# q of all four tiles ahead of k, smaller first transfers, and later z2 weights, in the opening of a fused attention and gMLP kernel

## The chip, the cores and the metric

One core of one Trainium2 chip. The metric is device time in microseconds (us) of one execution. A kernel is run several times; a timed comparison alternates it with the kernel before on the same chip. One execution of each is also profiled. Its span, as the profile prints it, is 1.7 to 1.9 us shorter than the same execution's device time.

Three engines matter here: TensorE (PE in the profile; PEld is its weight load), VectorE (DVE) and ScalarE (ACT). SyncE (SP) issues nearly all DMAs.

## The reference

With `x` of 2048 rows by 512 columns, normalised to `xn`, the result is the sum of `x` and two branches.

```python
xn = layernorm(x)
# A: sliding dilated attention, 32 heads of 16, window 8, dilation 2
q, k, v = xn @ wqkv;  o = softmax(q . k[window] / 4) v[window];  A = o @ wo
# B: gMLP
z = gelu(xn @ w_in);  z1, z2 = halves of z (688 columns each);  z2 = layernorm(z2)
B = (z1 * (w_sp @ z2 + b_sp)) @ w_out
out = x + A + B
```

## The kernel before

All of the program is ordered by hand. The 16 row tiles (128 rows each) form four "blocks" of four tiles (`j` is the block, `tb` the tile in it). The opening loads x and weights, normalises block 0, transposes it on TensorE and projects q and k of it. Then it does the same for block 1, whose last two tiles are transposed by DMA instead. After that the first matmuls with the z2 weights follow, and from there on a fixed list of steps.

```python
for tb in range(2):                       # first two x tiles, half on each DMA-issuing engine
    load_x0(SP, tb, 0); load_x0(A, tb, 1)
for tb in range(2, TB):
    A.dma_start(xall[:, 0, tb], xblk[0][:, tb])
load_wqk(SP, 0, 0, 2)                     # q weights, two transfers of 256 rows
load_wqk(SP, 0, 2, 4)
SP.dma_start(xall[:, 1, 0:2], xblk[1][:, 0:2])
load_wqk(SP, 1)                           # k weights, 512 KB
SP.dma_start(xall[:, 1, 2:4], xblk[1][:, 2:4])
for j in range(2, 4):
    SP.dma_start(xall[:, j], xblk[j])
SP.dma_start(w_z2[:], ...)                # z2 weights, 688 KB
# ... cut ...
def tr_copy(i, pt, c0=0, c1=C):           # ScalarE takes a transposed tile out of PSUM
    A.copy(xnT[:, c0:c1, i*P:(i+1)*P], pt[:, c0:c1, :])
def tr_dma(i):                            # or the tile is transposed by DMA
    SP.dma_start_transpose(xnT[:, :, i*P:(i+1)*P], xall[:, j, tb, :])
# qk_part(pq, j, m, b0, b1): projection m of block j for its tiles b0..b1; m 0,1 are q, m 2,3 are k
# ... cut ...
warm_up(10)                               # 10 matmuls of 512 columns on zeros
# ... cut: block 0, tiles 0 to 3 normalised; tiles 0 and 1 transposed ...
qk_part(pqs[0], 0, 0, 0, 2, kcs=range(2)); qk_part(pqs[0], 0, 0, 0, 2, kcs=range(2, 4))
tr_copy(t0[2], tr(t0[2]))
qk_part(pqs[1], 0, 1, 0, 2, (0,))
tr_copy(t0[3], tr(t0[3]))
qk_part(pqs[1], 0, 1, 0, 2, (1,))
qk_part(pqs[2], 0, 2, 0, 2)               # k of tiles 0 and 1: needs the k weights
# ... cut: statistics of block 1 ...
for n in range(2):
    qk_part(pqs[n], 0, n, 2, 4)           # q of tiles 2 and 3
    qk_copy(pqs[n], 0, n)
# ... cut: rest of block 0, transposes of block 1, block 1's projections, first z matmuls ...
```

Of the kernel before, what the change touches and what calls it, by code (L numbers as in the profile page):

```python
# [15 lines left out]
P = 128  # L16
# [3 lines left out]
TB = 4  # L20
TBS = 512
C = D // P
# [5 lines left out]
F = 1376  # L28
FH = 688
# [42 lines left out]
def kernel(  # L72
# [13 lines left out]
    V = nc.vector  # L86
# [3 lines left out]
    SP = nc.sync  # L90
# [3 lines left out]
    xblk = x2.rearrange("(b j p) d -> j p b d", b=TB, j=4)  # L94
# [9 lines left out]
    xall = r_x[:, 0:4 * TB * D].rearrange("p (j b d) -> p j b d", j=4, b=TB)  # L104
# [33 lines left out]
    xnT = sb.tile([P, C, S], BF16, name="xnT")  # L138
    w_z2 = sb.tile([P, C, FH], BF16, name="w_z2")
# [30 lines left out]
    def load_wqk(E, s, k0=0, k1=C):  # L170
        E.dma_start(wqk[:, s, k0:k1],
                    A_wqkv[:, s * D:(s + 1) * D].rearrange("(k p) f -> p k f", p=P)[:, k0:k1])
# [3 lines left out]
        load_x0(A, tb, 1)  # L176
    for tb in range(2, TB):
        A.dma_start(xall[:, 0, tb], xblk[0][:, tb])
    load_wqk(SP, 0, 0, 2)
    load_wqk(SP, 0, 2, 4)  # L180
    SP.dma_start(xall[:, 1, 0:2], xblk[1][:, 0:2])  # L181
    load_wqk(SP, 1)
    SP.dma_start(xall[:, 1, 2:4], xblk[1][:, 2:4])
    for j in range(2, 4):
        SP.dma_start(xall[:, j], xblk[j])
    SP.dma_start(w_z2[:], B_w_in[:, FH:F].rearrange("(k p) f -> p k f", p=P))


    V.memset(warm[:, 0:P], 0.0)
# [17 lines left out]
    def ln_stats(i, parts=1):  # L207
        j, tb = i % 4, i // 4
        w = D // parts
        for h in range(parts):  # L210
            V.bn_stats(stats[:, i, 6 * h:6 * h + 6], xall[:, j, tb, w * h:w * h + w])  # L211
        V.bn_aggr(mv[:, i, :], stats[:, i, 0:6 * parts])

    def ln_sqrt(sl):
        A.activation(rstd[:, sl], mv[:, sl, 1], ACT.Sqrt, bias=eps_t[:])

    def ln_recip(sl):
        V.reciprocal(rstd[:, sl], rstd[:, sl])

    def ln_apply(i):  # L220
        j, tb = i % 4, i // 4
        V.tensor_scalar(xall[:, j, tb, :], xall[:, j, tb, :], mv[:, i, 0:1], rstd[:, i:i + 1],
                        ALU.subtract, ALU.mult)

    def tr(i):
        j, tb = i % 4, i // 4
        pt = ps_aux.tile([P, C, P], BF16, name="pt", tag="aux")
        for c in range(C):
            PE.transpose(pt[:, c, :], xall[:, j, tb, c * P:(c + 1) * P], ident[:])  # L229
        return pt  # L230

    def tr_copy(i, pt, c0=0, c1=C):
        A.copy(xnT[:, c0:c1, i * P:(i + 1) * P], pt[:, c0:c1, :])

    def tr_dma(i):
        j, tb = i % 4, i // 4
        SP.dma_start_transpose(xnT[:, :, i * P:(i + 1) * P], xall[:, j, tb, :])
# [70 lines left out]
    def qk_part(pq, j, m, b0, b1, ccs=(0, 1), p0=None, kcs=range(C)):  # L308
        sd, c0 = m // 2, 2 * (m % 2)
        p0 = b0 if p0 is None else p0  # L310
        xv = xnT[:].rearrange("p k (b j t) -> p k b j t", b=TB, j=4)
        for cc in ccs:
            for kc in kcs:
                PE.matmul(pq[:, cc, p0 * P:(p0 + b1 - b0) * P], wqk[:, sd, kc, c0 + cc:D:C],  # L314
                          xv[:, kc, b0:b1, j, :], start=(kc == 0), stop=(kc == C - 1))

    def qk_copy(pq, j, m, b0=0, b1=TB, p0=None):
        sd, c0 = m // 2, 2 * (m % 2)
        p0 = b0 if p0 is None else p0
        if sd == 0:  # L320
            dst = qs[:, j, c0:c0 + 2, b0 * P:b1 * P].rearrange("p c (b t) -> p c b t", b=b1 - b0)
        else:
            dst = ks[:, c0:c0 + 2, HALO:HALO + S].rearrange("p c (b j t) -> p c b j t", b=TB, j=4)[:, :, b0:b1, j, :]
        cast = A.copy(dst, pq[:, :, p0 * P:(p0 + b1 - b0) * P].rearrange("p c (b t) -> p c b t", b=b1 - b0))  # L324
        if sd == 1:
            for i in k_reads[j]:
                tc.declare_no_dep(cast.ins, i, reason="other token columns of the same rows")
            k_casts[j].append(cast.ins)

    def qk_tile():  # L330
        return ps_mm.tile([P, 2, TBS], F32, name="pq", tag="mm")
# [219 lines left out]
    def blk(j):  # L551
        return [4 * tb + j for tb in range(TB)]

    def col(i):
        return slice(i, i + 1)
# [9 lines left out]
    def ln_tile(i):  # L565
        ln_recip(col(i))
        ln_apply(i)

    t0, i1 = blk(0), blk(1)
# [5 lines left out]
    for n in range(2):  # L575
        ln_tile(t0[n])
    tr_copy(t0[0], tr(t0[0]))
    pt1 = tr(t0[1])
    tr_copy(t0[1], pt1, 0, 2)
    tr_copy(t0[1], pt1, 2, 4)  # L580
    warm_up(1)
    warm_up(1, 2)
# [5 lines left out]
    pqs = [qk_tile() for _ in range(3)]  # L588
    qk_part(pqs[0], 0, 0, 0, 2, kcs=range(2))
    qk_part(pqs[0], 0, 0, 0, 2, kcs=range(2, 4))  # L590
    tr_copy(t0[2], tr(t0[2]))
    qk_part(pqs[1], 0, 1, 0, 2, (0,))
    tr_copy(t0[3], tr(t0[3]))
    qk_part(pqs[1], 0, 1, 0, 2, (1,))
    qk_part(pqs[2], 0, 2, 0, 2)
    for n in range(2):
        ln_stats(i1[n])
    ln_sqrt(slice(1, 8, 4))
    ln_stats(i1[2])
    ln_recip(slice(1, 8, 4))  # L600
    ln_apply(i1[0])
    ln_apply(i1[1])
    ln_stats(i1[3])
    for n in range(2):
        qk_part(pqs[n], 0, n, 2, 4)
        qk_copy(pqs[n], 0, n)
    ln_sqrt(slice(9, 16, 4))
    ln_stats(i2[0])
    ln_recip(slice(9, 16, 4))
    for n in range(2, 4):  # L610
        ln_apply(i1[n])
        tr_dma(i1[n])
    qk_part(pqs[2], 0, 2, 2, 4, (0,))
    tr_copy(i1[0], tr(i1[0]))
    qk_part(pqs[2], 0, 2, 2, 4, (1,))
    tr_copy(i1[1], tr(i1[1]))
    qk_copy(pqs[2], 0, 2)
    pq3 = qk_tile()
    qk_part(pq3, 0, 3, 0, 4)
    qk_copy(pq3, 0, 3)  # L620
    for n in range(1, 4):
        ln_stats(i2[n])
    ln_sqrt(blk_cols(2))
# [7 lines left out]
    pqs = [qk_tile() for _ in range(3)]  # L631
# [79 lines left out]
```

## Time and profile before

| | before |
|---|---|
| timed, median of 3 | 203.11 us (202.99 to 203.35) |
| the profiled execution | 204.07 us, span 202.2 us |
| TensorE busy | 97% of the span |
| chain of waits | 92% TensorE |

From the page of the kernel before, the busy times (us, share of the span, instructions) and the engines of the chain of waits:

```profile
...
PE 196.5 (97%) x1667; PEld 124.5 (62%) x1667; DVE 186.4 (92%) x269; ACT 106.8 (53%) x174; POOL 4.0 (2%) x14
...
PE 92%; DMA 5%; DVE 1%; issue 0%; SPq 0%
...
```

The chain of waits of the kernel before in the first 45 us (start, length, what):

```profile
...
3.64 6.73 DMA r_w<-in_A_wqkv_dram
...
10.42 3.25 PE pq L314 x28
13.67 0.22 PE pt L229 x4
13.89 0.44 PE pq L314 x4
14.33 0.22 PE pt L229 x4
14.55 4.35 PE pq L314 x32
18.90 0.87 PE pa L314 x8
19.77 3.49 PE pq L314 x32
23.27 3.50 PE pz L243 x24
...
```

What TensorE waited for in the kernel before from 6 to 24 us (total, times, longest):

```profile
...
PE pq L314 <- DMA r_w<-in_A_wqkv_dram: 0.9, 1, 0.9
...
```

The chain reads as follows: the k weights were issued at 3.64 us and took 6.73 us to land. From 10.42 us TensorE works without a break through the projections (`pq`, `pa`), and reaches the first z matmul (`pz`) at 23.27 us. Before 10.42 us it stood 0.9 us, waiting for these weights. A chain that is TensorE from there to the end says that only the opening can be shortened.

### The profile page before, as it was taken

Reading aid. Unit: us, or ns where it says so; the run is one execution under the profiler, and the core shown is the slowest. Engines: PE = TensorE matmul, PEld = TensorE weight load, DVE = VectorE, ACT = ScalarE, POOL = GpSimd, SP = SyncE. Lnnn points to the kernel's source line nnn. Section 1 sums busy time; section 2 is a strip of 40 time slices with the busy share of each in tenths; the row PEclk is TensorE's granted clock in tenths of the full one; section 3 lists DMA queues with packets and bytes.
Section 4 is the critical chain, followed back from the end, with each engine's and each line's share of the span. In section 5 each row is a group of like instructions: output and inputs, shape, how many; then the busy total and the mean of one; then the engine's idle time right before and its main releaser. Section 6 shows DMA issues by size and latency. Waiting matters only on the chain.

```text
span 202.2 us, 4055 instructions
## 1 busy us (share of the span) xinstructions
PE 196.5 (97%) x1667; PEld 124.5 (62%) x1667; DVE 186.4 (92%) x269; ACT 106.8 (53%) x174; POOL 4.0 (2%) x14
## 2 busy tenths in 40 slices
PE   7799999999999999999999999999999999999994
PEld 2589856646656666666656666644666446664562
DVE  5979799999999999999979999999999999999814
ACT  3565999889999886081383285134712152131400
POOL 3000000400000000000000000000000000000000
PEclk9999999999999999999999999999999999999999
DMA  5982557000895000759939908990243996059373
GB/s 154 339 272 55 104 104 249 0 0 0 133 201 87 0 3 0 135 167 231 220 81 199 223 5 203 201 211 7 77 104 85 249 188 90 0 148 189 84 221 110
DMA packets 66338, 25.91 MB, mean 128 GB/s; under 512 B 56272, under 2 KB 66064, under 8 KB 66064
## 3 DMA queue, kind: packets, MB, share of 16 engines
q1 hardware_dynamic: 65600, 25.19, 55.0%
q10 hardware_dynamic: 720, 0.47, 0.7%
q8 instruction: 13, 0.21, 0.5%
q14 instruction: 5, 0.04, 0.1%
HBM read 10.13 MB, written 2.10 MB: 60 GB/s over the span
## 4 chain that ended last, share of the span: by engine, by line
PE 92%; DMA 5%; DVE 1%; issue 0%; SPq 0%
PE pg L457 37%; PE pz L243 19%; PE pq L314 13%; PE po L535 8%; PE pv L418 7%; PE po L505 6%; DMA r_w<-in_A_wqkv_dram 3%; DMA r_x<-in_A_x_dram 1%; PE pl L368 1%; DVE r_pr L523 1%; PE po L514 1%; PE pb L505 1%; PE pa L314 0%; PE pt L229 0%; SPq L181 0%
## 5 line engine op out<-in xcount | busy, mean ns | idle before, releaser
L457 PE MATMUL pg<-z,r_qk 128*128 128x344 bf16 x448 | 66.6, 309 | 0.0
L457 PEld LDWEIGHTS <-r_qk 128*128 128x128 bf16 x448 | 43.8, 98 | 21.8
L243 PE MATMUL pz<-w_z,xnT 128*128 128x344 bf16 x256 | 40.0, 309 | 0.0
L432 DVE TENSOR_TENSOR r_pr<-r_x,r_w 128x2048 bf16<-128x2048 bf16 x32 | 38.5, 1220 | 0.3
L463 ACT ACTIVATE gs<-pg,b_col 128x688 bf16<-128x688 f32 x16 | 13.2, 834 | 48.2 <-PE pg L457 48.2
L436 DVE TENSOR_TENSOR r_pr<-r_pr 128x2048 bf16<-128x2048 bf16 x28 | 34.1, 1219 | 0.4
L243 PEld LDWEIGHTS <-xnT 128*128 128x128 bf16 x256 | 24.6, 98 | 14.4 <-issue 1.9
L314 PE MATMUL pq<-xnT,r_w 128*128 128x256 bf16 (+1 forms) x176 | 29.0, 316 | 1.0 <-DMA r_w<-in_A_wqkv_dram 0.9
L348 DVE TENSOR_TENSOR r_pr<-r_qk 128x2048 bf16<-128x2048 bf16 x24 | 28.3, 1220 | 0.1
L314 PEld LDWEIGHTS <-r_w 128*128 128x128 bf16 x184 | 20.1, 114 | 8.2 <-DMA r_w<-in_A_wqkv_dram 1.1
L324 ACT CAST r_qk<-pq 128x1024 bf16<-128x1024 f32 (+1 forms) x16 | 15.4, 989 | 2.9 <-PE pq L314 2.9
L535 PE MATMUL po<-r_w,r_uz 128*128 128x512 bf16 x70 | 16.0, 379 | 0.0
L305 ACT ACTIVATE r_uz<-pz 128x688 bf16<-128x688 f32 x16 | 11.7, 742 | 7.3 <-PE pz L243 7.2
L505 PE MATMUL po<-r_lg,r_pr 32*128 32x512 bf16 x224 | 14.5, 375 | 0.0
L518 ACT CAST r_qk<-po 128x512 bf16<-128x512 f32 x12 | 6.4, 589 | 14.7 <-PE po L535 14.6
L418 PE MATMUL pv<-xnT,r_w 128*32 128x512 bf16 x256 | 14.2, 379 | 0.0
L535 PEld LDWEIGHTS <-r_uz 128*128 128x128 bf16 x85 | 8.1, 98 | 9.3 <-issue 1.1
L357 DVE TENSOR_TENSOR r_pr<-r_pr 128x4096 bf16<-128x4096 bf16 x6 | 13.6, 2287 | 0.0
L211 DVE BATCH_NORM_STATS2 stats<-r_x 128x6 f32<-128x512 bf16 (+1 forms) x18 | 10.9, 613 | 2.2 <-DMA r_x<-in_A_x_dram 2.2
L267 ACT ACTIVATE junk<-z 128x688 bf16<-128x688 bf16 x16 | 12.4, 776 | 0.1
L418 PEld LDWEIGHTS <-r_w 128*32 128x32 bf16 x256 | 9.5, 138 | 4.4
L261 ACT ACTIVATE z<-pz 128x688 bf16<-128x688 f32 x16 | 11.8, 737 | 0.8 <-PE pz L243 0.7
(83 smaller groups left out, 175.4 us busy)
## 6 DMA issues: line engine op xcount, KB each, us to landing
r_lg<-in_A_wo_dram SPq DMA_DIRECT2D x8, 256.0 KB, 3.9
r_qk<-in_A_x_dram SPq DMA_DIRECT2D x12, 128.0 KB, 2.3
out_dram<-r_qk SPq DMA_DIRECT2D x12, 128.0 KB, 2.8
w_z<-in_B_w_in_dram SPq DMA_DIRECT2D x2, 688.0 KB, 5.4
r_w<-in_A_wqkv_dram SPq DMA_DIRECT2D x2, 512.0 KB, 5.4
r_x<-in_A_x_dram SPq DMA_DIRECT2D x2, 512.0 KB
r_w<-in_B_w_out_dram SPq DMA_DIRECT2D x1, 640.0 KB, 5.7
r_w<-in_A_wqkv_dram SPq DMA_DIRECT2D x2, 256.0 KB, 4.5
```

What stands on the lines that cost most here:

```text
L243: PE.matmul(pz[:, hh, 0:FHALF], xnT[:, kc, i * P:(i + 1) * P], wz[:, kc, hh * FHALF:(hh + 1) * FHALF], start=(kc == 0), stop=(kc == C - 1))
L314: PE.matmul(pq[:, cc, p0 * P:(p0 + b1 - b0) * P], wqk[:, sd, kc, c0 + cc:D:C], xv[:, kc, b0:b1, j, :], start=(kc == 0), stop=(kc == C - 1))
L324: cast = A.copy(dst, pq[:, :, p0 * P:(p0 + b1 - b0) * P].rearrange("p c (b t) -> p c b t", b=b1 - b0))
L348: prod = V.tensor_tensor(pr[g % 3][:, c].rearrange("p w b t -> p b w t"), q3.unsqueeze(2).broadcast_to([P, TB, 4, P]), k4, ALU.mult)
L357: V.tensor_tensor(pr[g % 3][:, 0:2], pr[g % 3][:, 0:2], pr[g % 3][:, 2:4], ALU.add)
L418: PE.matmul(pv[32 * tb:32 * tb + 32, dd, :], wv[:, kc, 2 * d2 + dd, :], xnT[:, kc, tb * TBS:(tb + 1) * TBS], start=(kc == 0), stop=(kc == ...
L432: V.tensor_tensor(pw_t[n], vp[:, :, off:off + P], a_sb[:, slot_w(w), ts].unsqueeze(1).broadcast_to([P, DH, P]), ALU.mult)
L436: V.tensor_tensor(pw_t[n] if dst is None else dst, pw_t[n], pw_t[m], ALU.add)
L457: PE.matmul(pg[:, hh, 0:FHALF], wsp[n][:, k, :], z2[:, k, hh * FHALF:(hh + 1) * FHALF], start=(k == 0), stop=(k == NT - 1))
L463: A.activation(gs[:], tiles.pop(("g", n))[:, :, 0:FHALF], ACT.Identity, bias=b_col[:, i:i + 1])
L505: PE.matmul(pc, op[32 * tb:32 * tb + 32, d, o * P:(o + 1) * P], wo_r[32 * tb:32 * tb + 32, d, cs], start=(d == 8), stop=False, tile_positi ...
L535: PE.matmul(pc, uT[:, o % 2, m, tb * P:(tb + 1) * P], wout[:, m, cs], start=False, stop=(m == MCH - 3))
```

## The change

Three parts. (1) TensorE takes q of all four tiles of block 0 before any k, so it has work while the k weights travel; k is then done in 512-column matmuls. VectorE takes half of tile 3 out of PSUM, and square roots are done per tile. (2) The q weights and block 1's x come in transfers of 128 rows. (3) The z2 weights are issued behind the two DMA transposes of block 1.

```diff
@@ -176,14 +176,14 @@
         load_x0(A, tb, 1)
     for tb in range(2, TB):
         A.dma_start(xall[:, 0, tb], xblk[0][:, tb])
-    load_wqk(SP, 0, 0, 2)
-    load_wqk(SP, 0, 2, 4)
-    SP.dma_start(xall[:, 1, 0:2], xblk[1][:, 0:2])
-    load_wqk(SP, 1)
-    SP.dma_start(xall[:, 1, 2:4], xblk[1][:, 2:4])
+    for kc in range(C):
+        load_wqk(SP, 0, kc, kc + 1)
+    for tb in range(TB):
+        if tb == 2:
+            load_wqk(SP, 1)
+        SP.dma_start(xall[:, 1, tb], xblk[1][:, tb])
     for j in range(2, 4):
         SP.dma_start(xall[:, j], xblk[j])
-    SP.dma_start(w_z2[:], B_w_in[:, FH:F].rearrange("(k p) f -> p k f", p=P))
 
 
     V.memset(warm[:, 0:P], 0.0)
@@ -231,6 +231,9 @@
 
     def tr_copy(i, pt, c0=0, c1=C):
         A.copy(xnT[:, c0:c1, i * P:(i + 1) * P], pt[:, c0:c1, :])
+
+    def tr_copy_v(i, pt, c0, c1):
+        V.tensor_copy(xnT[:, c0:c1, i * P:(i + 1) * P], pt[:, c0:c1, :])
 
     def tr_dma(i):
         j, tb = i % 4, i // 4
@@ -588,36 +591,38 @@
     pqs = [qk_tile() for _ in range(3)]
     qk_part(pqs[0], 0, 0, 0, 2, kcs=range(2))
     qk_part(pqs[0], 0, 0, 0, 2, kcs=range(2, 4))
+    qk_part(pqs[1], 0, 1, 0, 2, (0,))
     tr_copy(t0[2], tr(t0[2]))
-    qk_part(pqs[1], 0, 1, 0, 2, (0,))
-    tr_copy(t0[3], tr(t0[3]))
-    qk_part(pqs[1], 0, 1, 0, 2, (1,))
-    qk_part(pqs[2], 0, 2, 0, 2)
+    qk_part(pqs[1], 0, 1, 0, 2, (1,), kcs=range(2))
+    pt3 = tr(t0[3])
+    qk_part(pqs[1], 0, 1, 0, 2, (1,), kcs=range(2, 4))
+    tr_copy_v(t0[3], pt3, 0, 2)
+    tr_copy(t0[3], pt3, 2, 4)
+    qk_part(pqs[0], 0, 0, 2, 4, kcs=range(2))
+    qk_part(pqs[0], 0, 0, 2, 4, kcs=range(2, 4))
+    qk_part(pqs[1], 0, 1, 2, 4)
     for n in range(2):
         ln_stats(i1[n])
-    ln_sqrt(slice(1, 8, 4))
-    ln_stats(i1[2])
-    ln_recip(slice(1, 8, 4))
-    ln_apply(i1[0])
-    ln_apply(i1[1])
-    ln_stats(i1[3])
+        ln_sqrt(col(i1[n]))
     for n in range(2):
-        qk_part(pqs[n], 0, n, 2, 4)
+        ln_tile(i1[n])
         qk_copy(pqs[n], 0, n)
-    ln_sqrt(slice(9, 16, 4))
+    qk_part(pqs[2], 0, 2, 0, 4)
+    for n in range(2, 4):
+        ln_stats(i1[n])
+        ln_sqrt(col(i1[n]))
+    for n in range(2, 4):
+        ln_tile(i1[n])
+        tr_dma(i1[n])
+    SP.dma_start(w_z2[:], B_w_in[:, FH:F].rearrange("(k p) f -> p k f", p=P))
+    tr_copy(i1[0], tr(i1[0]))
+    pq3 = qk_tile()
+    qk_part(pq3, 0, 3, 0, 4, (0,))
+    tr_copy(i1[1], tr(i1[1]))
+    qk_part(pq3, 0, 3, 0, 4, (1,))
+    qk_copy(pqs[2], 0, 2)
+    qk_copy(pq3, 0, 3)
     ln_stats(i2[0])
-    ln_recip(slice(9, 16, 4))
-    for n in range(2, 4):
-        ln_apply(i1[n])
-        tr_dma(i1[n])
-    qk_part(pqs[2], 0, 2, 2, 4, (0,))
-    tr_copy(i1[0], tr(i1[0]))
-    qk_part(pqs[2], 0, 2, 2, 4, (1,))
-    tr_copy(i1[1], tr(i1[1]))
-    qk_copy(pqs[2], 0, 2)
-    pq3 = qk_tile()
-    qk_part(pq3, 0, 3, 0, 4)
-    qk_copy(pq3, 0, 3)
     for n in range(1, 4):
         ln_stats(i2[n])
     ln_sqrt(blk_cols(2))
```

In instruction counts, TensorE has 3318 matmuls and weight loads in place of 3334: eight pairs of weight load and matmul fewer, because the first half of block 0's k is done in 8 matmuls of 512 columns in place of 16 of 256.

## The prediction

> **What bounds the kernel now.** TensorE. The page gives PE 97% of a 202.2 us span, and the chain of waits is 92% PE. In the table by stages PE is full from 15 us until the tail. The only slack a prologue change can win lies before about 10.4 us: in the chain, PE works without a break from 10.42 us, and what it waited for there is the DMA of the k weights (issued at 3.64, landed at 10.37; 0.9 us of PE idle). By then PE has done 16 of block 0's projection matmuls (256 wide).
>
> **Costs read from the trace.** A 256-wide projection matmul 0.11-0.12 us apart (28 took 3.25 us), a 512-wide one 0.22; four transposes 0.22; ScalarE copy of a transposed tile 0.59 us, of half a tile 0.38; cast of 128x1024 1.0; VectorE statistics of a tile about 0.8, apply 0.41; one DMA transpose occupies the issuing queue 1.3 us and lands 2.4 us after its issue; one load issue about 0.45 us.
>
> **What changes.**
> 1. Order of PE: q of all four tiles first (32 matmuls of 256), then k in 512-wide matmuls. So PE has 16 matmuls more that do not need the k weights. I expect tile 3's halves copied at about 9.4 (VectorE) and 9.8 us (ScalarE), q finished near 11.2 us instead of 12.2, and the k weights there before that. From 11.2, k (1.74), two transposes (0.44) and the last k (1.74) end near 15.1 us, where before block 1's projections began at 16.3: 1.2 us won.
> 2. Transfers in 128-row pieces: same bytes in the same order. Eight DMA semaphores are used in turn, so the k-weight load now waits for the third x tile and issues near 5.3 us instead of 3.64. [...] the packet records show it saturated near 350 GB/s from 4.5 us; its turn comes only at about 6.6-7. So I expect it to land still at 10-10.7 us. ([...] here a load's completions spread by over 1 us.)
> 3. The z2 weights (688 KB) issue near 17 us behind block 1's two transposes and land near 21. They are needed at about 22.3 us (23.1 before). About 1 us of slack.
> 4. ScalarE and VectorE: per-tile square roots put the first two tr copies of block 1 near 14.1-15.2, so PE may wait 0.1-0.2 us there. Block 2's normalisation stays where it was (18.8-18.95), so its four DMA transposes still land by about 25.7, just when PE, 1 us earlier, wants them.
>
> VectorE's block 3 normalisation waits for a square root behind PE-paced casts, so the products also start about 1 us earlier. So the gain should survive, less the waits of point 4.
>
> **Predicted**: 202.2 us, 0.9 less; range 201.5 to 203.0. Faster by over 2%: 0.01; within 2%: 0.98; slower by over 2%: 0.01.
>
> **Signs.** No PE wait for the k weights, or under 0.3 us; first block 1 projection at 15.1-15.4 us instead of 16.3; first z matmul at 22.2-22.5 us instead of 23.1; VectorE's first product near 24.3 instead of 25.28; no PE wait for the z2 weights.
>
> **What would make it wrong.** The k weights landing after 11.2 us (late issue starves the queue): each us late costs one. The z2 weights landing after 22.4, or holding up block 2's transposes, gives the gain back at q of block 2. Or later stages tied to VectorE or loads that do not move: then about 203.

Point 2: "it" is the load queue there, and "its turn" that of the k weights. That this turn comes at 6.6-7, behind the loads issued before, was my estimate, and the "10-10.7" rests on it. What the traces of before and after show is this. In both, the last completions of SyncE's loads up to 8 us (10 in before, 13 in after) come in the order of issue. In before the queues moved 323 to 354 GB/s from 4.5 to 6.5 us, at a DMA share of 0.93 to 1.03; the 16 completions of the k weights came from 8.02 to 10.37 us, and TensorE went on at 10.42. The DMA issues name eight semaphores in turn: in after the load of the k weights has that of the third x tile, whose last completion is at 5.51 us, and issues at 5.53. The sum was the 1.2 us won by the order, less the waits of point 4, put at 0.9 us.

## The result, and the profile after

| | before | after |
|---|---|---|
| timed, 6 runs each, same rounds | 203.1 us (202.99 to 203.82) | 204.0 us (203.4 to 204.25) |
| profiled execution, span | 202.2 us | 201.7 us |

The ratio is 1.0034 (95% interval 1.0014 to 1.0054): slower by a third of a percent, where I had forecast 0.9 us less. A ratio is the mean time of one kernel's fast runs over that of the other's of the same rounds, so it is not quite the ratio of the medians quoted.

The two traces point the other way from the times: the span after is 0.5 us shorter. So neither trace shows a typical execution. The profiled execution of before (204.07 us) was above all its six timed ones, and that of after (203.4 us) was the fastest of its six.

The chain of waits after, first 60 us (answering to the one of before):

```profile
...
14.15 0.41 DVE r_x L222
14.57 0.61 DVE stats L211
15.20 0.18 DVE mv L212
15.38 0.09 DVE stats L211
15.47 3.57 DMA xnT<-r_x
19.04 0.05 issue
19.08 3.69 PE pq L317 x32
22.77 3.50 PE pz L246 x24
...
```

TensorE's wait for a DMA after, same stretch and columns as above:

```profile
...
PE pq L317 <- DMA xnT<-r_x: 0.2, 1, 0.2
...
```

The wait for the k weights is gone, as intended. In its place the chain runs over VectorE (`r_x L222`, the normalisation of block 1) into a DMA transpose `xnT<-r_x`, 3.57 us long, that TensorE waits for before the second half of block 1's projections at 19.08 us.

The load queue in the stretch from 5 to 10 us of the kernel before (length, then busy us and instructions of PE, PEld, DVE, ACT, POOL, granted clock, mean busy DMA engines, GB/s):

```profile
...
5.00:10.00 5.00, 3.69 (x35) 2.66 (x34) 4.75 (x15) 3.04 (x8) 0.00 (x0) 1.00 1.00 338
...
```

The same stretch after:

```profile
...
5.00:10.00 5.00, 4.15 (x41) 3.21 (x41) 4.29 (x14) 2.83 (x8) 0.00 (x0) 1.00 0.81 244
...
```

The small transfers leave the queue less full, 244 GB/s in place of 338, as I feared. But TensorE lost nothing by it here.

### The profile page after: what moved, and what is told of

Same layout as the page of the kernel before. It is cut to its first block, busy times and chain, and to the rows that moved or that the text cites. A ratio compares the mean times of both kernels' runs of the same rounds, so it can differ in the third digit from the quotient of the medians.

```text
span 201.7 us, 4045 instructions
## 1 busy us (share of the span) xinstructions
PE 196.1 (97%) x1655; PEld 123.4 (61%) x1659; DVE 186.7 (93%) x272; ACT 107.1 (53%) x176; POOL 3.5 (2%) x14
## 4 chain that ended last, share of the span: by engine, by line
PE 89%; DVE 5%; DMA 3%; issue 1%; ACT 0%
PE pg L460 37%; PE pz L246 19%; PE pq L317 10%; PE po L538 7%; PE pv L421 7%; PE po L508 6%; DVE stats L211 2%; DMA xnT<-r_x 2%; DMA r_x<-in_A_x_dram 1%; PE pl L371 1%; DVE r_x L222 1%; DVE r_pr L526 1%; PE po L517 1%; PE pb L508 1%; DVE mv L212 1%
## 5 line engine op out<-in xcount | busy, mean ns | idle before, releaser
L246 PEld LDWEIGHTS <-xnT 128*128 128x128 bf16 x256 | 24.6, 98 | 14.4 <-issue 1.9
L317 PEld LDWEIGHTS <-r_w 128*128 128x128 bf16 x176 | 19.1, 114 | 8.6 <-DMA xnT<-r_x 0.4
L327 ACT CAST r_qk<-pq 128x1024 bf16<-128x1024 f32 (+1 forms) x16 | 15.4, 988 | 1.4 <-PE pq L317 1.4
L538 PE MATMUL po<-r_w,r_uz 128*128 128x512 bf16 x66 | 15.1, 379 | 0.5 <-issue 0.5
```

Source lines behind the costliest of these rows:

```text
L246: PE.matmul(pz[:, hh, 0:FHALF], xnT[:, kc, i * P:(i + 1) * P], wz[:, kc, hh * FHALF:(hh + 1) * FHALF], start=(kc == 0), stop=(kc == C - 1))
L317: PE.matmul(pq[:, cc, p0 * P:(p0 + b1 - b0) * P], wqk[:, sd, kc, c0 + cc:D:C], xv[:, kc, b0:b1, j, :], start=(kc == 0), stop=(kc == C - 1))
L327: cast = A.copy(dst, pq[:, :, p0 * P:(p0 + b1 - b0) * P].rearrange("p c (b t) -> p c b t", b=b1 - b0))
L538: PE.matmul(pc, uT[:, o % 2, m, tb * P:(tb + 1) * P], wout[:, m, cs], start=False, stop=(m == MCH - 3))
```

## The experiments

The one measure that serves all of them: in each of the 14 traces, span minus the start of the first z matmul is 178.90 to 178.97 us. Whatever changed the time did so before the first z matmul. So one number per trace, that start, and the waits ahead of it tell where the time went.

### First call: is either trace typical, and what do the small transfers do?

Two kernels unchanged; `split_only` is before with only part 2:

```diff
-    load_wqk(SP, 0, 0, 2)
-    load_wqk(SP, 0, 2, 4)
-    SP.dma_start(xall[:, 1, 0:2], xblk[1][:, 0:2])
-    load_wqk(SP, 1)
-    SP.dma_start(xall[:, 1, 2:4], xblk[1][:, 2:4])
+    for kc in range(C):
+        load_wqk(SP, 0, kc, kc + 1)
+    for tb in range(TB):
+        if tb == 2:
+            load_wqk(SP, 1)
+        SP.dma_start(xall[:, 1, tb], xblk[1][:, tb])
```

`after_whole` is after with the same lines the other way round.

`before_again` was to show this:

> The kernel before, unchanged. The profiled execution of before took 204.07 us where its timed runs have a median of 203.1; so its trace may be an unlucky one. Theory A (the 0.9 us wait of TensorE for the k weights is an accident of that one trace): this trace has a span near 201.3 us and a wait for the k weights of under 0.3 us, because they land near 9.4-9.6 us instead of 10.37. Theory B (the wait is in every run): again 0.7 us or more of wait and a span near 202.

Measured: span 201.5 us, wait for the k weights 0.3 us. The timed runs are 203.23 us in the median (ratio 0.9998). TensorE's wait in this second trace of before:

```profile
...
PE pq L314 <- DMA r_w<-in_A_wqkv_dram: 0.3, 1, 0.3
...
```

The weights came at 9.7 us in place of 10.4. Span, wait and landing lie just outside the figures of Theory A and far from those of Theory B. So a wait is in both traces, but its 0.9 us in the first was three times that of the second. The semaphore updates in the traces show where it comes from: a load has 16 completions in these traces, and in the first trace of before 15 of those of the k weights had come by 9.37 us and the last at 10.37 (9.59 and 9.69 in the second). The long wait was for one late completion. None of the instruction transfers of the sections below runs at that time. Eleven more timed runs of before lie between 202.89 and 204.58 us: the kernel before scatters widely.

> The kernel after, unchanged. Its profiled execution (203.4 us) was the fastest of six whose median is 204.0. Theory A: its trace was a lucky one; here the span is 202.0-202.4 and the start of the first z matmul is 0.3-0.7 us later than 22.6 us, with a wait of TensorE for a DMA (k weights or the DMA transposes of block 1) that was 0.2 us in the first trace. Theory B: the trace repeats, and the loss is in something the profile hides.

Measured: span 202.0, ratio 1.0013 (0.9981 to 1.0045), 203.81 us. The chain of waits after, second trace:

```profile
...
15.35 4.00 DMA xnT<-r_x
19.34 0.04 issue
19.39 3.69 PE pq L317 x32
23.08 1.02 PE pz L246 x7
```

TensorE's wait in it:

```profile
...
PE pq L317 <- DMA xnT<-r_x: 0.8, 1, 0.8
...
```

The wait for the DMA transpose, 0.2 us in the first trace of after, is 0.8 us here. The theory that the first trace was a lucky one held.

> Before with only the 128-row transfers. Theory A (the small transfers, whose issues wait for semaphores of earlier ones, leave the load queue underfed: 244 GB/s in 5-10 us in the trace after against 338 before): slower than before by 0.5-1.5 us, k weights landing after 10.4 us in every trace. Rival (the loss comes from the new order of work or from the late z2 weights): equal to before within 0.2 us.

Measured: 204.11 us against 203.53, ratio 1.0023 (0.9994 to 1.0052), not clear of noise. The cause I expected failed in the trace: the wait for the k weights was only 0.2 us, and the time went in a 0.9 us wait for a DMA transpose of block 1, as in after:

```profile
...
PE pq L315 <- DMA xnT<-r_x: 0.9, 1, 0.9
...
PE pq L315 <- DMA r_w<-in_A_wqkv_dram: 0.2, 1, 0.2
```

> After with the transfers of before (256-row pieces) and all else as after. Theory A: the loss goes; equal to before or up to 0.8 us faster (202.3-203.1). Rival: as slow as after, about 0.9 us over before.

Measured: 204.04 us against 203.53, ratio 1.0019 (0.9988 to 1.0049), with a 0.6 us wait for the transpose. So the size of the transfers was not what made after slow, and my first theory fell.

### A new theory, from the DMA records

The transposes of block 1 were late, so I looked at what else their DMA engines did. The transfers in the stretch 15 to 19.5 us of the second trace of after (queue and kind: packets, MB, share; then the issues, with median time to landing):

```profile
...
q8 instruction: 1, 0.02, 1.3%
q14 instruction: 1, 0.01, 0.6%
...
xnT<-r_x SPq DMA_TRANSPOSE x3, 3.8
```

The same stretch of the second trace of before:

```profile
...
q14 instruction: 1, 0.01, 0.4%
...
xnT<-r_x SPq DMA_TRANSPOSE x3, 2.4
```

In the median of these issues a transposed tile lands 2.4 us after its issue in before and 3.8 us in after (4.0 for the one that TensorE waited for; the other landing known in after, 3.6 us, is of a transpose of block 2 that travels beside the z2 weights), and after has one transfer on a queue marked "instruction", `q8`, in this stretch that before does not have. In the packet records of the trace it is a single packet of 16 KB. It begins at 16.10 us and takes 0.93 us. From 17.1 us on, five packets of 256 bytes of the second transpose then take 0.56 to 0.72 us each, where their usual time is 0.02 us (in the first trace of after five such packets, from 17.25 us on, take 0.69 to 0.85 us). In before the same packet begins at 14.1 to 14.4 us, ahead of the transposes. (These times count from the zero of the chains above. The recorded expectations below count packets from a zero 0.3 us earlier, so 0.3 us has to be taken off the refill times that they name.)

A whole run has 13 of these packets, for 3334 matmuls and weight loads, so one per 256 (3334/13 = 256.5; the recorded text below says 3336). From one packet to the next TensorE starts 128 to 130 pairs on average in each of the 14 traces (129.1 in the first trace of before and 127.6 in that of after, by the weight loads). So I took each for a refill of TensorE's instructions, and call it a refill from here on. This rests on the count alone; the packet records name no engine. Before the first z matmul, every wait of TensorE over 0.15 us in these traces is put down to an engine or a data transfer, none to a refill; what would have to be shown is that the cost falls on a neighbour's transfer.

Theory I: the first refill falls on block 1's transposes in the new order. To test it, move the refill and nothing else. Cutting warm-up matmuls into narrower ones puts more TensorE instructions ahead of it, with the same number of columns:

```diff
-    warm_up(10)
+    warm_up(6)
+    warm_up(16, 1)
```

### Second call: move the refill; undo the other parts

> After with 4 of the 10 first warm-up matmuls (512 wide) cut into 16 of 128: 12 more TensorE instruction pairs early, same columns of warm-up, nothing else. In the three traces with the new order a 16 KB instruction transfer (the page's queue 8) of 0.9-1.1 us begins at 16.4-16.7 us and packets of block 1's second DMA transpose then stand still for 0.6-0.8 us; TensorE waits 0.2-0.8 us for that transpose. In before the same transfer begins at 14.4-14.7, ahead of the transposes. There are 13 of these for 3336 TensorE instructions, one per 256. Theory I (the new order needs 8 instruction pairs fewer, so the refill came later, onto the transpose): here the refill begins at 13.8-15 us, no slow packets in the transposes, no wait for them, first z matmul at 22.2-22.5, span 201.1-201.5, time 0.4-0.9 us below after. Theory II (the transposes are late for another reason, such as the queue or the issue): refill moves but the wait of 0.6 us stays, time as after.

Measured: 202.98 us (202.84 to 203.04) against 203.46, ratio 0.9975 (0.9955 to 0.9995). The refill begins at 13.41 us, just ahead of the expected stretch, no packet of the transposes was slow, and the wait is gone from the chain:

```profile
...
14.48 3.54 PE pq L317 x28
18.02 0.87 PE pa L317 x8
18.90 3.49 PE pq L317 x32
22.39 1.75 PE pz L246 x12
```

Its transfers from 15 to 19.5 us, in which no packet of queue 8 appears:

```profile
...
q14 instruction: 1, 0.01, 0.9%
...
xnT<-r_x SPq DMA_TRANSPOSE x3, 2.5
```

The transposed tiles land 2.5 us after issue again, and the one that TensorE needs was issued no earlier than in after (15.62 us, and 15.47 in the first trace of after). This is as Theory I said, and Theory II falls.

> Control: before with the same cut of the warm-up. Its refill comes ahead of the transposes already, so both theories expect the time of before within 0.2 us; refill at 13.3-14.2. If this is faster than before too, the cut helps by itself and the first run of this call proves nothing.

Measured: 203.51 us against 203.46, ratio 1.0011 (0.9981 to 1.0042): the cut by itself does nothing clear of noise for before, and the interval leaves it at most 0.2%. The profiled execution happened to be a long one (204.88 us), and shows why before scatters:

```profile
...
PE pq L314 <- DMA r_w<-in_A_wqkv_dram: 1.8, 1, 1.8
...
```

The wait for the k weights was 1.8 us in it: 15 of their 16 completions had come by 8.99 us and the last at 11.32. (Its refill came at 14.59 us, later than I had expected, with the whole order of work 1.8 us late.)

> After with the z2 weights loaded where before loads them. Theory I: the refill still falls on the second transpose, wait of 0.2-0.8 us, time as after within 0.3 us. Rival III (the z2 weights, issued right behind the transposes, hold them or block 2's up): the wait goes and it is 0.5-0.9 us faster than after.

```diff
     for j in range(2, 4):
         SP.dma_start(xall[:, j], xblk[j])
+    SP.dma_start(w_z2[:], ...)
@@
-    SP.dma_start(w_z2[:], ...)      # behind tr_dma of block 1
```

Measured: 204.04 us against 203.46, ratio 1.0024 (1.0001 to 1.0048). The refill is at 16.11 us, the wait for the transpose 1.0 us. The rival that blamed the late z2 weights falls.

> The new order of work alone: transfers whole and z2 weights early as in before. Theory I: refill near 16.5 us on the transposes, time as after within 0.3 us (203.7-204.2). If the loss came from the transfers or the z2 weights instead, this is at or below before (203.0).

This is after with both edits undone (whole transfers, z2 weights early). Measured: 204.28 us against 203.46, ratio 1.0035 (1.0013 to 1.0057), refill at 16.12 us, wait 1.0 us. So the new order of work alone has the loss of after. From its chain:

```profile
...
15.61 4.24 DMA xnT<-r_x
19.84 0.05 issue
19.89 3.68 PE pq L317 x32
...
```

### Third call: dose, parts and a better kernel

`after_pe4` has `warm_up(6); warm_up(8, 2)` in place of `warm_up(10)`: four more pairs.

> Dose: after with only 4 more TensorE instruction pairs (4 warm-ups of 512 as 8 of 256). Theory I: the refill comes 0.5-1 us earlier than in after, at 15.4-16.0 us, so it now falls on the first of block 1's two DMA transposes (data 15.6-16.6); slow packets there, the second delayed behind it, TensorE still waits 0.3-1.0 us; time like after (203.6-204.3), not like the run with 12 more (202.98). If more early instructions helped by themselves, this would win about a third of it (203.6 or less) with no wait.

Measured: 203.1 us against 203.45, ratio 0.9974 (0.9958 to 0.9989). The expectation failed: the refill came at 13.34 us, not at the expected 15.4 to 16.0 (15.1 to 15.7 in the zero used here), and there was no wait for the transposes. Four pairs moved it as far as twelve (13.41 us). Where the refill goes, the wait goes with it, as Theory I says; but its time is no linear function of the instruction count. What gives such a jump no run shows.

> The new order of work alone (transfers whole, z2 weights early) with the 12 more pairs. Theory I says the order carries the gain and the 128-row transfers and the late z2 weights are worth little: 202.9-203.2, no wait for the transposes. If the transfers or the late z2 weights carry it: as order_only (204.3) or at least 0.4 us above the run of after with 12 more pairs.

Measured: 203.13 us against 203.45, ratio 0.9987 (0.9965 to 1.0008); refill at 13.67 us, no wait for the transposes, span 201.2. The last of the k weights' completions came as late as 10.66 us in this trace (the 15 others by 9.16), and TensorE did not wait: here q first did what it was meant to do. Compared with `order_only` (1.0035), moving the refill is worth about as much as in after (0.5%, in other rounds). Against `after_pe12` (0.9975), the intervals overlap; what parts 2 and 3 are worth is not settled, and it is at most a few tenths of a us.

> Before with only the 128-row transfers, and the 12 more pairs. In the run without them the refill at 15.5 us fell on the first transpose (wait of 0.9 us). Theory I: refill at 13.5-14.5, wait for the transposes gone; the wait for the k weights stays, since this order still needs them by 9.5 us; time 203.0-203.6, 0.5-1 us below the run of the transfers alone (204.1). If the small transfers themselves starve the load queue: 204 again, with a wait for the k weights over 0.5 us.

Measured: 203.63 us against 203.45, ratio 1.0005 (0.9981 to 1.003). The wait for the transposes is gone, as Theory I said. But the refill came at 14.77 us, later than expected and only 0.4 us earlier than in `split_only`; in this execution the transposes were issued 1 us later (first one at 15.70 us, and 14.71 in `split_only`), so it is as much they that moved. The profiled execution (204.39 us) waited 1.3 us for the k weights, which is the sign that the rival gave; but its time was among the longest of its own set, and before itself shows such waits. Whether the small transfers delay the k weights stays open.

`after_pe11` has `warm_up(5); warm_up(16, 1)`.

> Candidate: after with one 512-wide warm-up less than in the run with 12 more pairs (5 of 512 and 16 of 128, so 11 more pairs than after). In that run the warm-ups ended at 5.5 us, 0.1-0.2 later than the first transposes were ready. Expected 202.8-203.0, 0.1 us below 202.98; refill at 13.8-14.5, no wait for the transposes.

Measured: 202.89 us (202.8 to 203.21) against 203.45, ratio 0.9969 (0.9954 to 0.9984), refill at 13.44 us, no wait for the transposes. This is the best version tried: 0.3% under before, and 1.1 us under the 204.0 of after, which was measured in other rounds.

### All traces side by side

Refill start is that of the first 16 KB instruction packet in the packet records; waits are TensorE's, in us.

| trace | span | first z matmul | wait for k weights | wait for block 1's transposes | refill starts |
|---|---|---|---|---|---|
| before | 202.2 | 23.27 | 0.9 | 0 | 14.39 |
| before_again | 201.5 | 22.57 | 0.3 | 0 | 14.09 |
| before_pe12 | 203.2 | 24.21 | 1.8 | 0 | 14.59 |
| split_pe12 | 202.7 | 23.76 | 1.3 | 0 | 14.77 |
| split_only | 202.8 | 23.89 | 0.2 | 0.9 | 15.18 |
| after | 201.7 | 22.77 | 0 | 0.2 | 16.36 |
| after_again | 202.0 | 23.08 | 0 | 0.8 | 16.10 |
| after_whole | 202.2 | 23.25 | 0 | 0.6 | 16.25 |
| after_z2_early | 202.5 | 23.63 | 0 | 1.0 | 16.11 |
| order_only | 202.5 | 23.57 | 0 | 1.0 | 16.12 |
| after_pe4 | 201.0 | 22.06 | 0 | 0 | 13.34 |
| after_pe11 | 201.0 | 22.10 | 0 | 0 | 13.44 |
| after_pe12 | 201.3 | 22.39 | 0 | 0 | 13.41 |
| order_pe12 | 201.2 | 22.22 | 0 | 0 | 13.67 |

In the traces with q first, the wait for the k weights is 0. In the six traces where the refill began between 15.1 and 16.4 us, there is a wait for block 1's transposes; in the eight others there is none. Closer still: in these six the refill began 0.5 to 2.3 us after the first of block 1's transposes was issued, and in the eight others 0.4 to 1.6 us before it. In the chains of the six, the transpose that TensorE waited for lands 3.35 to 4.27 us after its issue. Undisturbed, in the first trace of before and in `after_pe12`, it is 2.4 to 2.6 us (of which the issue takes 1.2 to 1.3). In before and its kin, span minus the wait for the k weights is nearly constant: 202.2 - 0.9, 201.5 - 0.3, 203.2 - 1.8 and 202.7 - 1.3 give 201.2 to 201.4.

## Why the prediction was wrong

**TensorE as the bound, and only the opening to win: right.** Span minus the first z matmul stayed at 178.9 us in every trace.

**Point 1, the order: the mechanism was right, its size was not.** "1.2 us won", with block 1's projections at 15.1 instead of 16.3, took the start of before from one trace and the total from the median of others. After did begin block 1's projections at about 15.2 us (in its timeline a group of 28 projection matmuls starts at 14.33, and the first four, of 0.22 us, are the last of k). But that trace of before ran 204.07 us, 1 us over the median that I subtracted from. In the second trace of before the wait was 0.3 us and not 0.9, and the same point came near 15.6 us (18.21 less 24 matmuls of 0.11). So the term "0.9 us of PE idle" was mis-sized for a typical run. With the refill out of the way, the measured gain is 0.25 to 0.3% (0.9975, 0.9974 and 0.9969), 0.5 to 0.6 us, and not 0.9; with the new order alone (0.9987) it is not clear of noise.

**Point 2, the transfers: right in effect.** The k-weight issue did come later (5.53 us, and 3.64 in before) and the queue was less full (244 GB/s from 5 to 10 us, and 338). In the first trace of after the weight load ahead of the first k waited 0.23 us for the k weights at 11.26 us, so they landed later than my "10-10.7"; TensorE's matmuls did not wait. No run here shows that the small transfers help, and with or without them the loss was there.

**Point 3, the z2 weights: right.** Their last data came at 20.9 us in the first trace of after and at 21.6 in the second, and the load's completion at 21.5 and 22.1, against "near 21", and TensorE did not wait for them.

**Point 4 was looking at the wrong transposes.** It watched "Block 2's" four DMA transposes and took it that block 1's two would land after the 2.4 us that a transpose took in before. This is the step that failed, the cost "lands 2.4 us after its issue" taken over for them: the one that TensorE needed landed 3.57 us after issue in the first trace of after and 4.0 in the second, because the first instruction refill now fell on them. Eight pairs of TensorE instructions fewer, and the new order of waits, moved the refill (which of the two, no run separates) from 14.1-14.4 to 16.1-16.4 us. Moving it away again took the ratio from 1.0034 to 0.9975, 0.6% or 1.2 us; these two are of different rounds, but `order_only` (1.0035) stood beside the 0.9975 in the same ones.

**The sum.** Predicted was 202.2, measured 204.0, so 1.8 us off. The refill's collision makes about 1.2 us of it (0.8 if one takes the 1.0013 of `after_again`). The rest, about 0.6 us, agrees with what the wait of 0.3 us in the second trace of before falls short of the 0.9 us that I read in the first. Another way to see it: the forecast "1.2 us won", taken from the 204.07 us of the execution that it was read in, gives 202.9 us, and the new order without the collision ran 202.89 to 203.13 us. This split is worked out from such numbers; no run measured it by itself. Of the signs, the k weights, block 1's projections and the z2 weights were right. VectorE's first product came at 24.77 us and not near 24.3. The first z matmul at 22.2-22.5 us was meant by the timeline, which has it 0.16 us earlier than the chain of the table: 22.61 and 22.91 us in the two traces of after, so missed, and 21.90 to 22.23 in the runs of the new order that moved the refill. It was a poor sign, for the second trace of before (22.41) meets it too.

One effect I had not forecast: with q first and the refill out of the way, the times stop scattering. `after_pe12` has 202.84 to 203.04 us, and before in the same rounds 203.05 to 204.56. (Of the 24 timed runs of the four such kernels one, of `order_pe12`, was at 204.21; the rest end at 203.40.)

**What stays open:** what sets the instant of the refill; how a single packet of 16 KB holds up the whole transpose (the runs show that the delay goes when the refill is moved, not the steps between); why one completion of the k weights comes late in some runs, so that the wait for them in before and its kin differs from 0.3 to 1.8 us; and what parts 2 and 3 are worth by themselves.

## What to carry to other kernels

Before subtracting a wait that a trace shows from a timed median, check that the profiled execution itself ran at the median; if it did not, profile again, because a wait on a DMA can differ from run to run (here 0.9 and 0.3 us for the same kernel). When a tuned opening gets a new order and loses time in a DMA that should not have changed, look for instruction transfers among its neighbours in the DMA records: moving a few instructions forward, at no cost in work, can move a refill off a transfer that is on the critical path (here four to twelve pairs of weight load and matmul more moved its start from 16.1-16.4 to 13.3-13.7 us, and the wait of 0.2 to 1.0 us was gone). Measure from a fixed point (here, the first z matmul) to see at once which part of the run a difference comes from.
